# Folding a feature map into a weight matrix by halves of TensorE's rows, in a pass whose order is written out by hand

## The chip, the cores and the metric

The kernel runs on one core of a Trainium2 chip. The metric is the device time of one execution in microseconds (us). A profile shows one execution, recorded by the hardware, with an instruction's engine, start and length. The engines are TensorE (PE; its weight loads are listed apart as PEld), VectorE (DVE), ScalarE (ACT), GpSimd (POOL) and SyncE (SP), which issues most DMAs. "Lnnn" is a line of the kernel.

## What is computed

A transformer layer on x of 2048 tokens by 512 channels, in float32: a linear attention with 32 heads of 16 channels, then a token-mixing MLP (2048 to 1792 to 2048), both behind layernorms and with residuals. The change lies in the attention:

```python
q, k, v = heads of layernorm(x) @ wqkv
pq, pk  = q @ w_phi, k @ w_phi                      # a 16 x 16 matrix for each head
phi_q   = concat(softmax(pq), softmax(-pq))         # and phi_k alike
kv, z   = phi_k^T v, sum over tokens of phi_k
o       = (phi_q kv) / (phi_q z + 1e-6)
h       = x + o @ wo
out     = h + mixer(layernorm(h))
```

## The kernel before

Tokens are in 16 tiles of 128. Products that need float32 accuracy are made of parts: a matrix is split into a high part (fp32r) and the rest, and `mm3` (L69) adds three matmuls, high by high, high by low and low by high, of 128 rows by 512 moving columns each (L71, L72, L73).

**Preparation (L281 to L423).** The twelve chunks of `wT`, 128 rows each (0 to 3 for q, 4 to 7 for k, 8 to 11 for v), are loaded, and `center` (L315) takes the mean of each row out, which stands for layernorm's mean. `fold` (L332) turns a chunk around and multiplies q's and k's by phi on the way: four matmuls in plain float32 a chunk, each with 128 rows, 128 weight columns (a block of the chunk) and 128 moving columns. The moving operand `ph` (L361) is block-diagonal, with eight heads' 16 x 16 matrices on its diagonal. v's chunks are only transposed (L339). A chunk's four results fill one bank of PSUM; `hi_w` (L344, ACT at L350) copies them into the high part and `lo_w` (L352, DVE) subtracts for the low part. Chunks 0 and 1 are folded at L414 to L422, ahead of the first pass, and chunks 2 and 3 by `fold_rest` (L432) in it. Their banks come from `ps_q`, which has two and serves q's projections later.

**The first pass (L424 to L461).** For each token tile: x is loaded twice, turned (`xraw`, L111) and straight (`xh`, L116); split into parts (ACT and POOL); the row's variance is made (L129, L130 on ACT, L132 on DVE, L133 on POOL); k's projection goes to PSUM (pool `ps_k`, two banks), and DVE takes maxima, minima and two differences from it (`logit_ops`, L161); ACT does the exponentials (L195), DVE sums and reciprocals (L217, L218), POOL the products and the running sum z (L219, L223); v's projection (`ps_v`, two banks) goes through ACT (L210). After four tiles `kv` (L225) adds their products into `kvp`, in matmuls of 128 rows and 32 weight columns, so that four lie side by side in the array. q's projections and logits of six tiles are put in between.

Here the order of PE is written out: `PASSES` (L27) is a list of steps that L457 to L461 run, and each step issues one tile's k, v or q work, or f, which is `fold_rest`. Inside that block the other engines' order is chosen by the scheduler, which weighs all instructions by costs and due times of its own. Up to L423 and from L463 on, the order of the program's text holds for all engines but, in the preparation, SP.

**The rest.** From L465 the first pass ends; a second pass (L829) makes the attention's output a tile at a time: `s_tr` (L593) transposes the features in two halves of 64 rows, which alternate (L598, 64 rows, 128 weight columns, 64 moving columns), `s_num` (L609) multiplies by kv in tiles of 64 rows by 32 columns (L616), and `s_wo` follows. Then comes the mixer (L1105), which takes about half of the time.

Of the kernel before, what the change touches and what calls it, by code (L numbers as in the profile page):

```python
# [9 lines left out]
F32 = mybir.dt.float32  # L10
F32R = mybir.dt.float32r
AF = mybir.ActivationFunctionType
# [5 lines left out]
P = 128  # L18
# [24 lines left out]
def block_kernel(ctx: ExitStack, tc: tile.TileContext, x, xT, wT, phic, wo, w1, b1, w2, b2,  # L43
# [63 lines left out]
    X, XH, EQ, PK, VS, SQ, PS, W = {}, {}, {}, {}, {}, {}, {}, {}  # L107

    def load_x(t):
        raw = kk.tile([P, KD, P], F32, name="xraw", bufs=3)  # L110
# [7 lines left out]
    def split_x(t, raw, alone=False):  # L118
# [4 lines left out]
        else:  # L123
            split(X[t][:, 0], X[t][:, 1], raw, nc.gpsimd)

    def stats_x(t):
        junk = kk.tile([P, D], F32, name="sqj", bufs=1)
        st = kk.tile([P, 2], F32, name="st")
        nc.scalar.activation(junk, XH[t], AF.Copy, scale=-1.0 / D, accum_out=st[:, 0:1])  # L129
        nc.scalar.activation(junk, XH[t], AF.Square, bias=st[:, 0:1], accum_out=st[:, 1:2])  # L130
        ve = kk.tile([P, 1], F32, name="ve")
        nc.vector.tensor_scalar(ve, st[:, 1:2], 1.0 / D, EPS, op0=ALU.mult, op1=ALU.add)  # L132
        nc.gpsimd.tensor_tensor(r1[:, t:t + 1], ve, mhalf[:, :1], op=ALU.pow)  # L133
# [27 lines left out]
    def logit_ops(src, e, pool):  # L161

        v = src.rearrange("p (j h d) -> p j h d", h=2, d=DH)
        ev = signs(e)
        mx = wk.tile([P, NPR, 2], F32, name="mx")
        mn = wk.tile([P, NPR, 2], F32, name="mn")

        def shift():
            nc.vector.tensor_sub(ev[:, :, 0], v, mx.unsqueeze(3).to_broadcast([P, NPR, 2, DH]))
            if pool:  # L170
                MN.append((ev, mx, mn))
            else:
                nc.vector.tensor_sub(ev[:, :, 1], mn.unsqueeze(3).to_broadcast([P, NPR, 2, DH]), v)  # L173

        return [lambda: nc.vector.tensor_reduce(mx, v, axis=AX.X, op=ALU.max),
                lambda: nc.vector.tensor_reduce(mn, v, axis=AX.X, op=ALU.min),
                shift]

    def negate():

# [9 lines left out]
    def run(*lists):  # L190
        for op in turns(*lists):
            op()

    def exps(t, e):
        nc.scalar.activation(e, e, AF.Exp, scale=r1[:, t:t + 1])  # L195

    def heads(e):
        return e.rearrange("p g (a d) -> p (g a) d", d=DH)

    def k_ops(t, o):  # L200
        PK[t] = kk.tile([P, NG, P], F32, name="pk", bufs=PKS)
        run(logit_ops(o, PK[t], False))

    def k_logits(t):
        k_ops(t, proj(t, wkh, wkl, ps_k, "pk_ps"))
        exps(t, PK[t])

    def v_out(t, o):
        VS[t] = kk.tile([P, D], F32, name="vs", bufs=5)
# [2 lines left out]
    def v_proj(t):  # L212
        v_out(t, proj(t, wvh, wvl, ps_v, "pv"))

    def k_norm(t, z=True):
        sk = wk.tile([P, 2 * H], F32, name="sk", bufs=2)
        nc.vector.reduce_sum(sk, heads(PK[t]), axis=AX.X)  # L217
        nc.vector.reciprocal(sk, sk)  # L218
        nc.gpsimd.tensor_mul(heads(PK[t]), heads(PK[t]), sk.unsqueeze(2).to_broadcast([P, 2 * H, DH]))  # L219
        if z and t == 0:  # L220
            nc.gpsimd.tensor_copy(zacc, PK[t])
        elif z:
            nc.gpsimd.tensor_add(zacc, zacc, PK[t])  # L223

    def kv(t):  # L225

# [54 lines left out]
    with tc.tile_pool(name="prep", bufs=1) as prep:  # L281
# [50 lines left out]
        def fold(c, pool, name):  # L332
            FO[c] = pool.tile([P, KD, P], F32, name=name, tag=name)
            for kt in range(KD):
                if c < 8:
                    nc.tensor.matmul(FO[c][:, kt, :], WR[c][:, kt * P:(kt + 1) * P], ph[:, c % 4, :],
                                     start=True, stop=True)
                else:
                    nc.tensor.transpose(FO[c][:, kt, :], WR[c][:, kt * P:(kt + 1) * P], ident)  # L339
# [4 lines left out]
        def hi_w(c, vector=False, halves=1):  # L344
            n = KD // halves
            for k in range(0, KD, n):
                if vector:
                    nc.vector.tensor_copy(parts(c)[0][:, k:k + n], FO[c][:, k:k + n])
                else:
                    nc.scalar.activation(parts(c)[0][:, k:k + n], FO[c][:, k:k + n], AF.Copy)  # L350

        def lo_w(c):  # L352
            hi, lo = parts(c)
            nc.vector.tensor_sub(lo, FO[c], hi)

        warm = ps_k.tile([P, P], F32, name="pk_ps", tag="pk_ps")
        for _ in range(WARM):
            nc.tensor.matmul(warm, ones, ones, start=True, stop=True)
        with tc.manual_schedule(engines={ET.PE, ET.DVE, ET.Activation, ET.Pool}):
# [63 lines left out]
            center(3, False)  # L423
        stats_x(3)  # L424
        exps(3, PK[3])
        load_h(4)
        stats_x(4)
        k_ops(4, k4)
        exps(4, PK[4])
        v_out(2, v2)  # L430
# [7 lines left out]
        def k_step(t):  # L438

            if t + 2 < NT:  # L440
                raw = load_x(t + 2)
                load_h(t + 2)
            if t > 4:
                k_logits(t)
            k_norm(t - 1)
            if t + 2 < NT:
                split_x(t + 2, raw)
                stats_x(t + 2)

        def q_step(_):  # L450
            q_mm()
            run(q_logits(0))
            q_exp(0)
            run(q_sums(0))
# [803 lines left out]
```

## The time and the profile before

| | |
|---|---|
| time, median of 3 runs | 516.41 us (516.18 to 516.86) |
| the profiled execution's own time | 516.23 us |
| its span, first to last instruction | 514.5 us |
| preparation, on PE | to about 34 us |
| first pass, in the part that the change orders by hand | about 34 to 114 us on PE |
| second pass | about 138 to 260 us |
| mixer | to the end |

"Busy" is time in which an engine had at least one instruction running, "idle before" what it sat idle ahead of a group, with the engine or DMA that ended it. In the timeline a row begins with the start and the length in us; "x16" puts sixteen instructions that follow each other into one row. A matmul's recorded length holds the way through the array, so that the next one starts before it ends: the distance of two starts is the price of one. A matmul in plain float32 leaves two records, each with a weight load; one in fp32r and a transpose leave one.

### The profile page before, as it was taken

The numbers are of one execution on the slowest core, as the hardware profiler recorded it, in microseconds if no ns is written. First come the engines' busy times: TensorE is split into PE (matmuls) and PEld (weight loads), VectorE is DVE, ScalarE is ACT, GpSimd is POOL, SyncE is SP. The second block draws the span as 40 slices with busy tenths as digits, with TensorE's granted clock in tenths as the row PEclk, the third lists the DMA queues.
The fourth block names the chain that finished last, engine by engine and source line by source line (L and its number), as shares of the span: only waits on it lengthen the run. The fifth ranks groups of instructions, "written<-read, shape, count | busy, mean of one in ns | idle before, by whom it ended". The sixth has DMA issues, their size and how long they took to land.

```text
span 514.5 us, 10292 instructions
## 1 busy us (share of the span) xinstructions
PE 509.4 (99%) x3954; PEld 439.7 (85%) x3954; DVE 432.5 (84%) x736; ACT 300.7 (58%) x530; POOL 247.1 (48%) x195
## 2 busy tenths in 40 slices
PE   9999999999999999999999999999999999999997
PEld 8888888888877777777788999988899999999997
DVE  6799889989887899699876878986789989968973
ACT  6999853526267878867675636555364434434530
POOL 3579997876999999975203330000002112211220
PEclk9999999999999999999999999999999999999999
DMA  8642301020113233443329784333425687668743
GB/s 306 218 143 84 103 22 42 1 77 8 43 62 103 81 104 126 147 160 126 103 79 256 152 194 120 103 103 102 143 63 126 162 194 172 128 152 192 168 63 71
DMA packets 52112, 61.76 MB, mean 120 GB/s; under 512 B 4704, under 2 KB 38752, under 8 KB 52064
## 3 DMA queue, kind: packets, MB, share of 16 engines
q1 hardware_dynamic: 45440, 52.43, 32.6%
q0 software_dynamic: 6336, 8.52, 12.1%
q8 instruction: 31, 0.51, 0.4%
q10 hardware_dynamic: 288, 0.17, 0.1%
q14 instruction: 17, 0.14, 0.1%
HBM read 49.96 MB, written 11.14 MB: 119 GB/s over the span
## 4 chain that ended last, share of the span: by engine, by line
PE 95%; DVE 2%; ACT 1%; issue 0%; DVEq 0%
PE py L951 22%; PE pu L71 10%; PE pu L72 9%; PE pu L73 9%; PE py L958 9%; PE py L960 4%; PE pk_ps L71 3%; PE pk_ps L72 3%; PE pk_ps L73 3%; PE pv L73 3%; PE pv L72 3%; PE pv L71 3%; PE po L71 3%; PE po L73 2%; PE po L72 2%; PE pn L616 2%
## 5 line engine op out<-in xcount | busy, mean ns | idle before, releaser
L66 ACT ACTIVATE wp<-wraw 128x896 fp32r<-128x896 f32 (+1 forms) x96 | 79.8, 869 | 83.4 <-DVE wraw L797 34.1
L67 DVE TENSOR_TENSOR wp<-wraw,wp 128x896 fp32r<-128x896 f32 (+1 forms) x96 | 92.3, 986 | 20.7 <-ACT wp L66 20.5
L1001 POOL DMA_DIRECT2D out<-u x28 | 24.5, 952 | 170.0 <-ACT u L1047 110.8
L951 PE MATMUL py<-cb,wp 128*128 128x256 f32 x582 | 79.8, 283 | 0.0
L951 PEld LDWEIGHTS py<-cb,wp 128*128 128x128 f32 x582 | 74.0, 191 | 0.0
L490 POOL TENSOR_TENSOR ez<-eq,zB 128x1024 f32<-128x1024 f32 x16 | 38.4, 2404 | 3.8 <-ACT zB L550 3.8
L71 PE MATMUL pu<-hs,wp 128*128 128x512 f32 x96 | 37.4, 389 | 0.0
L72 PE MATMUL pu<-hs,wp 128*128 128x512 f32 x96 | 37.4, 389 | 0.0
L73 PE MATMUL pu<-hs,wp 128*128 128x512 f32 x96 | 37.3, 389 | 0.0
L219 POOL TENSOR_TENSOR pk<-pk,sk 128x1024 f32<-128x1024 f32 x16 | 31.1, 1943 | 11.3 <-DVE sk L218 10.1
L958 PE MATMUL py<-cb,wp 128*128 128x512 f32 x126 | 36.1, 394 | 0.0
L514 POOL TENSOR_TENSOR eq<-eq,w 128x1024 f32<-128x1024 f32 x16 | 32.4, 2026 | 3.5 <-DVE w L511 3.5
L223 POOL TENSOR_TENSOR zacc<-zacc,pk 128x1024 f32<-128x1024 f32 x13 | 31.3, 2406 | 0.5
L783 POOL DMA_DIRECT2D wraw<-in_w x16 | 14.2, 970 | 31.7 <-DMA wraw<-in_w 21.3
L195 ACT ACTIVATE pk<-pk,r 128x1024 f32<-128x1024 f32 x16 | 18.4, 1148 | 15.0 <-DVE pk L173 14.4
L951 PE MATMUL py<-uf,wp 128*128 128x256 f32 x198 | 26.6, 283 | 0.0
L71 PE MATMUL pu<-wq,xs 128*128 128x512 f32 x64 | 26.1, 408 | 0.0
L71 PE MATMUL pu<-hs,whl 128*128 128x512 f32 x64 | 26.0, 406 | 0.0
L71 PE MATMUL po<-woh,oh 128*128 128x512 f32 x64 | 25.3, 395 | 0.1
L72 PE MATMUL pu<-wq,xs 128*128 128x512 f32 x64 | 25.0, 391 | 0.0
L72 PE MATMUL pu<-hs,whl 128*128 128x512 f32 x64 | 25.0, 390 | 0.0
L73 PE MATMUL po<-woh,ol 128*128 128x512 f32 x64 | 25.0, 390 | 0.0
(213 smaller groups left out, 1398.5 us busy)
## 6 DMA issues: line engine op xcount, KB each, us to landing
wraw<-in_w SPq DMA_DIRECT2D x112, 256.0 KB, 3.4
out<-u POOLq DMA_DIRECT2D x21, 256.0 KB, 5.2
xraw<-in_xT SPq DMA_DIRECT2D x16, 256.0 KB, 3.0
xh<-in_x SPq DMA_DIRECT2D x16, 256.0 KB, 2.6
h<-in_x SPq DMA_DIRECT2D x16, 256.0 KB, 2.8
out<-h SPq DMA_DIRECT2D x16, 256.0 KB, 2.0
wraw<-in_wT SPq DMA_DIRECT2D x12, 256.0 KB, 5.2
wraw<-in_w POOLq DMA_DIRECT2D x16, 128.0 KB, 3.9
```

The lines of the kernel that those rows point to most:

```text
L66: nc.scalar.activation(hi, src, AF.Copy)
L67: lo_engine.tensor_sub(lo, src, hi)
L71: nc.tensor.matmul(o, ah, bh, start=first, stop=False)
L72: nc.tensor.matmul(o, ah, bl, start=False, stop=False)
L73: return nc.tensor.matmul(o, al, bh, start=False, stop=last).ins
L219: nc.gpsimd.tensor_mul(heads(PK[t]), heads(PK[t]), sk.unsqueeze(2).to_broadcast([P, 2 * H, DH]))
L223: nc.gpsimd.tensor_add(zacc, zacc, PK[t])
L490: nc.gpsimd.tensor_mul(EZ[t], EQ[t], zB)
L514: nc.gpsimd.tensor_mul(heads(EQ[t]), heads(EQ[t]), W[t].rearrange("p g c h -> p (g c h)").unsqueeze(2).to_broadcast([P, 2 * H, DH]))
L951: nc.tensor.matmul(o, w[:, m[0]], x[:, y], start=opens and i == 0, stop=closes and i == 2, skip_group_check=True)
L958: nc.tensor.matmul(o, wh_[:, m[0]], x(m[1]), start=first, stop=False, skip_group_check=True)
L1001: nc.gpsimd.dma_start(out[t * P:(t + 1) * P, k * HD:], flat(a), accum_op=ALU.add)
```

## The change

Two things are edited.

*The fold of q's chunks.* `fold_pair(c)` takes the place of `fold(c)` and `fold(c + 1)`. Because `ph` is block-diagonal, the upper 64 rows of a chunk only reach the upper 64 output columns, and the lower the lower. So each block's matmul of 128 rows by 128 moving columns becomes two of 64 rows by 64 moving columns, one for each half of the rows, with the weights 128 columns wide as before. They are issued in turn, into two banks, one for each half of the rows of both chunks. `pair_hi` and `pair_lo` copy and subtract a bank at a time; a bank now holds one half (64 columns) of both chunks, so the copies' targets are runs of 64 elements. k's fold stays as it is.

*The order.* `PASSES` goes. `FIRST` lists 285 tokens, each one operation (on one engine, but for the compound ones) of one tile, and a table `DO` maps the letter to a function; a block that orders all five engines by hand runs them. The compound functions are cut into single operations for it (`stats_x` into four, `k_norm` into four, the second difference of `logit_ops` into its own). The order that results is the one that the scheduler had chosen, for SP and POOL entirely and for DVE up to the shapes above. On PE the fold of chunks 2 and 3 (F2) now stands behind k's projection of tile 6 (k6) and not ahead of it. On ACT the copies and the centering that belong to the folds stand a few places later:

```
before: ... L210 vs#2, L350, L129 tile 5, L350, L324 chunk 3, L195 tile 3, L130 tile 5, L330 chunk 3, L129 tile 6, L195 tile 4 ...
after:  ... L210 vs#2, L129 tile 5, L195 tile 3, L130 tile 5, L350, L350, L324 chunk 3, L129 tile 6, L330 chunk 3, L195 tile 4 ...
```

The diff, cut to its core (lines of the old kernel's numbering):

```diff
-PASSES = [(s[0], int(s[1:] or 0)) for s in
-          "k5 v f k6 v q k7 q v k8 v q v q k9 k10 v k11 q k12 v k13 v q k14 v".split()]
+FIRST = """
+X5 H4 X6 a5 X7 b5 a6 b6 H5 X8 X9 s3 a7 S3 b7 a8 H6 X10 u3 b8 l4 r3 s4 m4 n2 k5 S4 o2 H7 X11 x4 y4 s5 N2 v3 u4
+p2 e3 l5 r4 S5 m5 H8 n3 s6 x5 e4 k6 F2 u5 y5 r5 S6 N3 o3 H9 n4 p3 c2 v4 u6 s7 N4 c3 d2 z2 e5 d3 l6 S7 K0 m6 K1
...
+"""
...
+        HALVES = [slice(64 * r, 64 * r + 64) for r in range(2)]
+
+        def fold_pair(c):
+
+            FO[c] = [ps_q.tile([P, 2, KD, 64], F32, name="pu", tag="pu") for _ in range(2)]
+            for i in range(2):
+                for kt in range(KD):
+                    for r, rows in enumerate(HALVES):
+                        nc.tensor.matmul(FO[c][r][:, i, kt, :], WR[c + i][rows, kt * P:(kt + 1) * P],
+                                         ph[rows, c + i, rows], start=True, stop=True, skip_group_check=True)
+
+        def pair_part(w, c, r):
+            return w[:, :, c * P:(c + 2) * P].rearrange("p k (i r f) -> p r i k f", i=2, r=2)[:, r]
+
+        def pair_hi(c, r):
+            nc.scalar.activation(pair_part(wqh, c, r), FO[c][r], AF.Copy)
+
+        def pair_lo(c, r):
+            nc.vector.tensor_sub(pair_part(wql, c, r), FO[c][r], pair_part(wqh, c, r))
...
-            fold(0, ps_q, "pu")
-            fold(1, ps_q, "pu")
+            fold_pair(0)
...
-            hi_w(0)
-            hi_w(1)
-            lo_w(0)
-            lo_w(1)
+            for r in range(2):
+                pair_hi(0, r)
+            for r in range(2):
+                pair_lo(0, r)
...
-        def fold_rest():
-            for c in range(2, 4):
-                fold(c, ps_q, "pu")
-                hi_w(c)
-                lo_w(c)
...
+        DO = {
...
+            "k": k_mm, "l": lambda t: LO_K[t][0](), "m": lambda t: LO_K[t][1](),
...
+            "j": lambda t: run(q_sum(t)), "F": fold_pair, "c": lambda c: pair_hi(c - c % 2, c % 2), "d": lambda c: pair_lo(c - c % 2, c % 2),
+        }
+        with tc.manual_schedule(engines={ET.PE, ET.DVE, ET.Activation, ET.Pool, ET.SP}):
+            for token in FIRST.split():
+                DO[token[0]](int(token[1:]))
-        with tc.manual_schedule(engines={ET.PE}):
-            k_step(3)
-            k_step(4)
-            for name, n in PASSES:
-                {"k": k_step, "v": lambda _: v_kv(), "q": q_step, "f": lambda _: fold_rest()}[name](n)
```

More of the change, by code (lines that the diff above doesn't have):

```diff
@@ L198, in heads, with logit_list @@
         return e.rearrange("p g (a d) -> p (g a) d", d=DH)
+    def logit_list(t, o):
+        PK[t] = kk.tile([P, NG, P], F32, name="pk", bufs=PKS)
+        return logit_ops(o, PK[t], False)
     def k_ops(t, o):
[L201 to L206, printed above, removed]
+        run(logit_list(t, o))
     def v_out(t, o):
@@ L213, in v_proj, with norm_sum, norm_rec, norm_mul @@
         v_out(t, proj(t, wvh, wvl, ps_v, "pv"))
-    def k_norm(t, z=True):
[L216 to L223, printed above, removed]
+    def norm_sum(t):
+        SK[t] = wk.tile([P, 2 * H], F32, name="sk", bufs=2)
+        nc.vector.reduce_sum(SK[t], heads(PK[t]), axis=AX.X)
+    def norm_rec(t):
+        nc.vector.reciprocal(SK[t], SK[t])
+    def norm_mul(t):
+        nc.gpsimd.tensor_mul(heads(PK[t]), heads(PK[t]), SK[t].unsqueeze(2).to_broadcast([P, 2 * H, DH]))
+    def norm_z(t):
+        if t == 0:
+            nc.gpsimd.tensor_copy(zacc, PK[t])
+        else:
+            nc.gpsimd.tensor_add(zacc, zacc, PK[t])
+    def k_norm(t, z=True):
+        norm_sum(t)
+        norm_rec(t)
+        norm_mul(t)
+        if z:
+            norm_z(t)
     def kv(t):
@@ new lines, in k_mm, with v_mm, q_list, hi_x @@
+        def k_mm(t):
+            LO_K[t] = logit_list(t, proj(t, wkh, wkl, ps_k, "pk_ps"))
+        def v_mm(t):
+            PV[t] = proj(t, wvh, wvl, ps_v, "pv")
+        def q_list(n):
+            q_mm()
+            EQ[n] = big.tile([P, NG, P], F32, name="eq", tag="big")
+            LO_Q[n] = logit_ops(PS[n], EQ[n], False)
+        def hi_x(t):
+            X[t] = big.tile([P, 2, KD, P], F32R, name="xs", tag="big")
+            nc.scalar.activation(X[t][:, 0], xr[t], AF.Copy)
+        DO = {
+            "X": lambda t: xr.update({t: load_x(t)}), "H": load_h,
+            "a": hi_x, "b": lambda t: nc.gpsimd.tensor_sub(X[t][:, 1], xr[t], X[t][:, 0]),
+            "s": stats_sum, "S": stats_square, "u": stats_var, "r": stats_rstd,
+            "k": k_mm, "l": lambda t: LO_K[t][0](), "m": lambda t: LO_K[t][1](),
+            "x": lambda t: LO_K[t][2](), "y": lambda t: LO_K[t][3](), "e": lambda t: exps(t, PK[t]),
+            "n": norm_sum, "N": norm_rec, "p": norm_mul, "z": norm_z,
+            "v": v_mm, "o": lambda t: v_out(t, PV[t]), "K": kv,
+            "q": q_list, "f": lambda t: LO_Q[t][0](), "g": lambda t: LO_Q[t][1](),
+            "h": lambda t: LO_Q[t][2](), "i": lambda t: LO_Q[t][3](), "E": lambda t: exps(t, EQ[t]),
+            "j": lambda t: run(q_sum(t)), "F": fold_pair, "c": lambda c: pair_hi(c - c % 2, c % 2), "d": lambda c: pair_lo(c - c % 2, c % 2),
+        }
@@ L463, in block_kernel @@
+        with tc.manual_schedule(engines={ET.PE, ET.DVE, ET.Activation, ET.Pool, ET.SP}):
+            for token in FIRST.split():
+                DO[token[0]](int(token[1:]))
+        q.update(logits=Q_EARLY, exp=Q_EARLY, sum=Q_EARLY)
+        v = NT - 4
     ms = ExitStack()
```

58 lines of the change are left out of this document (26 added, 32 removed).

## The prediction

> **What bounds the kernel now.** I read the busy times first, then the chain of work that ended last, then the list of what TensorE waited for, then the busy time by stretches, and last the timeline around the edited matmuls.
>
> ```profile
> span 514.5 us, 10292 instructions
> PE 509.4 (99%) x3954; PEld 439.7 (85%) x3954; DVE 432.5 (84%) x736; ACT 300.7 (58%) x530; POOL 247.1 (48%) x195
> ...
> PE 95%; DVE 2%; ACT 1%; issue 0%; DVEq 0%
> ```
> ```profile
> PE pk_ps L358 <- DVE eps L62: 1.1, 1, 1.1
> PE pn L616 <- DVE h L641: 0.2, 1, 0.2
> PE pu L336 <- POOL ph L361: 0.2, 1, 0.2
> ```
> ```profile
> core 0: us, PE busy (x) PEld busy (x) DVE busy (x) ACT busy (x) POOL busy (x), PEclk, DMA share, GB/s
> 30.00:130.00 100.00, 100.00 (x815) 83.33 (x814) 90.97 (x149) 61.87 (x109) 85.04 (x56) 1.00 0.18 54
> ```
>
> TensorE is busy for 509.4 of 514.5 us and makes 95% of the chain. It waits visibly three times, 1.1 + 0.2 + 0.2 = 1.5 us in all, and of these only L616 comes after the start. The written order covers TensorE's work from about 34 to 114 us; between 30 and 130 us it is never idle, at the full clock. So there is no wait in the first pass for a better order to remove. The new order can only lose; a gain can come from TensorE's own work alone, and a change in that work reaches the end as it is.
>
> **What the change does to each queue.** In the instruction order of the two programs, SP's and POOL's queues are the same, all DMAs included. DVE's are the same up to the shape of the four L354 subtractions. ACT has the same instructions, a few of them in other places between 34 and 45 us. On PE two things change. Sixteen matmuls of 128 rows by 128 moving columns (chunks 0 to 3) become 32 of 64 rows by 64 moving columns, which alternate between the two row halves. And the second pair of chunks goes behind the 12 matmuls of k's tile 6, where it stood ahead of them. That the order is written out costs and gives nothing by itself, since it writes what the scheduler had chosen.
>
> **The price of the fold now.** The timeline of PE and of its weight loads around the first pair of chunks, then the durations by line (least, median, most, in ns):
>
> ```profile
> 32.43 0.39 PE L73 MATMUL pv<-wvh,xs 128*128 128x512 f32 x1
> 32.66 1.95 PE L336 MATMUL pu<-ph,wraw 128*128 128x128 f32 x16
> 34.36 0.48 PE L71 MATMUL pk_ps<-wkh,xs 128*128 128x512 f32 x1
> 34.67 0.40 PE L72 MATMUL pk_ps<-wkl,xs 128*128 128x512 f32 x1
> ```
> ```profile
> 34.33 0.19 PEld L71 LDWEIGHTS pk_ps<-wkh,xs 128*128 128x128 f32 x1
> 34.44 0.19 PEld L72 LDWEIGHTS pk_ps<-wkl,xs 128*128 128x128 f32 x1
> ```
> ```profile
> L336 PEld LDWEIGHTS pu<-ph,wraw x48: 186/192/192, 5.1 to 41.5; 128*128 128x128 f32 x48
> L336 PE MATMUL pu<-ph,wraw x48: 270/275/347, 5.1 to 41.6; 128*128 128x128 f32 x48
> ```
>
> Eight matmuls in plain f32 leave 16 records, two passes each, and each pass has a weight load of its own. One is 275 ns long, and sixteen lie within 1.95 us, so one starts every (1.95 - 0.275)/15 = 0.112 us. From the start of the last matmul before (32.43) to the start of the second one behind (34.67) a pair costs 2.24 us. That distance I work out again for the new form. Two things could set the 112 ns: streaming 128 columns, or the weight load.
>
> **The price of the new form.** No row of before shows an f32 product on 64 rows with 128 weight columns. The nearest on one side are the transposes of L598 (64 rows, 128 weight columns, 64 moving, two halves in turn), on the other L336 itself, and kvp's L231 shows 64 moving columns in f32 in two passes.
>
> ```profile
> 138.10 0.71 PE L598 MATMUL tr<-ident,eq 64*128 64x64 f32 x16
> 138.74 0.50 PE L71 MATMUL pu<-wq,xs 128*128 128x512 f32 x1
> 139.07 0.40 PE L72 MATMUL pu<-wq,xs 128*128 128x512 f32 x1
> ```
> ```profile
> 138.09 0.57 PEld L598 LDWEIGHTS tr<-ident,eq 64*128 64x128 f32 x16
> ```
> ```profile
> L598 PEld LDWEIGHTS tr<-ident,eq x256: 135/138/140, 138.1 to 248.7; 64*128 64x128 f32 x128
> L598 PE MATMUL tr<-ident,eq x256: 221/222/272, 138.1 to 248.8; 64*128 64x64 f32 x128
> ```
> ```profile
> L339 PEld LDWEIGHTS pu<-ident,wraw x8: 138/140/142, 14.3 to 15.2; 128*128 128x128 f32 x8
> ```
> ```profile
> 46.91 0.39 PE L73 MATMUL pv<-wvh,xs 128*128 128x512 f32 x1
> 47.23 1.99 PE L231 MATMUL kvp<-pk,vs 128*32 128x64 f32 x128
> 49.15 0.50 PE L71 MATMUL pu<-wq,xs 128*128 128x512 f32 x1
> 49.49 0.40 PE L72 MATMUL pu<-wq,xs 128*128 128x512 f32 x1
> ```
> ```profile
> 49.15 0.19 PEld L71 LDWEIGHTS pu<-wq,xs 128*128 128x128 f32 x1
> 49.26 0.19 PEld L72 LDWEIGHTS pu<-wq,xs 128*128 128x128 f32 x1
> ```
> ```profile
> L231 PEld LDWEIGHTS kvp<-pk,vs x512: 106/110/110, 47.2 to 137.9; 128*32 128x32 f32 x171
> ```
> ```profile
> L616 PEld LDWEIGHTS pn<-pht,small x512: 102/107/108, 141.9 to 254.9; 64*32 64x32 f32 x171
> ```
>
> Streaming: L231 runs 128 records in groups of four, 32 groups in 1.99 us with a last record of 219 ns, (1.99 - 0.22)/31 = 57 ns a group. So 64 moving columns take half of the 112 ns, and tiles side by side share them.
>
> Weight load: a load of 128 columns is recorded at 192 ns (L336), one of 32 columns at 110 (L231). The 82 ns between them over 96 columns is 0.85 ns a column, 109 ns for 128. The timeline says the same: where nothing covers it, the next load follows after 34.44 - 34.33 and 49.26 - 49.15 = 0.11 us. And the rows that a load covers change nothing: 110 ns for 128 rows and 107 for 64 (L231, L616), 140 and 138 (L339, L598). What is cheaper is the load of a transpose, 138 against 192 ns with the same 128 columns, and so L598 gets by with a step of (0.57 - 0.138)/7 = 62 ns for a pair of halves.
>
> In the change the weights of each half are still 128 columns wide (`WR[c + i][rows, kt * P:(kt + 1) * P]`), and it is a product, not a transpose. Each half takes 16 loads for a pair of chunks, as many as the full array took. If both halves load at once, as L598's do, a step of two records takes the larger of 57 (streaming) and about 112 ns (load). I take **112 ns**; the bounds are 57 to 62 (L231, L598) below and 224 (no overlap of the two loads) above. Half the moving columns then buy nothing.
>
> What comes on top is the change of the array's shape. Into L231 the step is 47.23 - 46.91 = 0.32 us, where L336 had 0.23. The first load, 0.11, has nothing beside it. Behind L598 the last record starts at 138.10 + 0.71 - 0.22 = 138.59, L71 0.15 later, and L72 another 0.33 later.
>
> New distance for a pair: 0.32 + 0.11 + 15 x 0.112 + 0.15 + 0.33 = **2.59 us**, against 2.24: **+0.35 us**. Two pairs: **+0.70 us**.
>
> **What is moved, and who waits.** ACT's row of the last centering stands first, then the queue of the second pair's halves in before:
>
> ```profile
> 38.55 0.72 ACT L330 ACTIVATE wraw<-wraw,mu 128x512 f32<-128x512 f32 x1
> 39.17 0.63 ACT L129 ACTIVATE sqj<-xh 128x512 f32<-128x512 f32 x1
> ...
> 43.31 0.59 ACT L350 ACTIVATE wq<-pu 128x512 fp32r<-128x512 f32 x1
> ```
> ```profile
> 43.86 1.22 DVE L354 TENSOR_TENSOR wq<-pu,wq 128x512 fp32r<-128x512 f32 x2
> ```
> ```profile
> 39.90 1.95 PE L336 MATMUL pu<-ph,wraw 128*128 128x128 f32 x16
> ```
>
> The second pair started at 39.90 and needs the centered chunk 3, done at 38.55 + 0.72 = 39.27. In the new order one more L129 (0.63) stands ahead of that centering, so it is done by about 39.9. But the pair itself now starts behind k's tile 6: 39.90 + 0.35 + 12 x 0.23 (32.66 - 32.43 for one) = 43.0. Three us of cover. It ends near 43.0 + 0.1 + 0.11 + 1.68 + 0.25 = 45.1; two ACT copies with one L129 between them (0.58 + 0.83 + 0.59) and one subtraction (0.67) end near 47.8, where before the two subtractions ended at 45.1. q's first matmul with the low part, L72, stood at 49.49 and comes at 50.19: 2.4 us to spare. Behind the later subtractions DVE's k logits of tiles 5 and 6 wait up to 2.7 us. DVE has 9 us idle in 100 in that stretch, and PE does not wait for it anywhere there, so I cost this at nothing. If that cover were gone, each us that the last subtraction is later than 50.2 would stop TensorE for one us. The four copies and the four subtractions keep their 512 elements a partition, now in runs of 64; if that changes their length, the same margin covers it.
>
> **The sum.** The profiled execution took 516.23 us for a span of 514.5; it lies 0.18 below the median of 516.41. On its own time: 516.23 + 0.70 = 516.93. On the median: **517.1 us**, 0.14% longer.
>
> **The rivals.**
>
> *Halves pay off.* If a load on 64 rows takes half as long, or is hidden, the step is L598's 62 ns: 0.32 + 0.05 + 15 x 0.062 + 0.15 + 0.33 = 1.78 us, 0.46 less than now for a pair, 0.92 for both: 515.5. With L231's 57 ns and a first load of 0.03 it is 1.69, 1.1 for both: 515.3. For it: L598 does run so. Against it: L598's loads are of the cheaper kind, and no pair of rows shows a load that is shorter for fewer rows. The Trainium skill, "TensorEngine Tiling (Array Packing)", section Overview, states that a small dimension of at most 64 gives a tiling factor of 2 and a speedup of up to 2 times; by it this rival would hold, and the load rows above speak for less.
>
> *Loads in turn (the slower side).* If the loads of the two halves follow each other, there are 31 steps of 0.112 in place of 15: 4.38 us a pair, +2.14, two pairs +4.3: 520.7. Loads that overlap only in part are enough: from a step of 0.123 up the time is over 0.2% longer (0.70 + 30 x 0.011 = 1.03 us). Against it: L598's 16 loads lie in 0.57 us, two every 62 ns, though each is as long as L339's load on all 128 rows.
>
> *It doesn't do what it says.* If the halves' matmuls run one after the other but their loads overlap, two times 57 ns fill the same 112 ns: the time is that of the forecast, and only the distance of the records tells.
>
> *The written order stalls.* The second pair's late subtractions stop q's first tile (2.4 us of margin), or DVE's backlog reaches PE later. A us or two: 518 to 519.
>
> **How the numbers follow.** Load-bound forecast 0.62 (with its look-alike), halves pay off 0.22, loads in turn 0.08, stall 0.05, something near zero 0.03. The forecast's own range is 516.7 to 517.6: 10 ns a step either way make 0.3 us, the four changes of shape another 0.1 to 0.2. The range of 8 in 10 has to take in the halves that pay off, and it leaves out the loads in turn and most stalls: 515.3 to 517.8. A difference of 0.2%, 1.03 us, is about what a measurement of this kernel can tell from no change. Faster by more (below 515.4) takes the best form of the paying halves: 0.1. Slower by more (above 517.4) takes the loads in turn, the stall, or a step of 0.123 or more: 0.28. The rest, 0.62, is within.
>
> **What would show it.** In the changed kernel's timeline the fold's 32 records of a pair should lie within some 2.1 us and not 1.2; its loads should last about 190 ns and not 140; the two halves of a step should start 3 to 7 ns apart; L231's and the projections' rows should not move; PE's list of waits should stay at 1.5 us. A fold of 1.2 us, loads of 140 ns, or any new wait of PE on DVE or ACT between 30 and 130 us would prove it wrong.

## The result and the profile after

The changed kernel takes 518.0 us (median of 11 runs, 517.54 to 519.18), the kernel before, measured beside it, 516.58 (11 runs, 516.18 to 517.16). The ratio is 1.0027, 95% interval 1.0019 to 1.0035: slower by 1.42 us, where 517.1 and +0.70 were forecast. The profiled execution took 517.72 us.

The page of the changed kernel, and TensorE's list of waits:

```profile
span 515.9 us, 10354 instructions
PE 511.1 (99%) x3986; PEld 440.7 (85%) x3986; DVE 432.7 (84%) x736; ACT 300.3 (58%) x530; POOL 247.2 (48%) x195
```
```profile
PE pk_ps L411 <- DVE eps L71: 1.1, 1, 1.1
PE pn L664 <- DVE h L689: 0.2, 1, 0.2
```

TensorE is the bound as before, with 32 matmul records more and no new wait. (Its third wait in before, 0.2 us of L336 for ph, is gone.) (L80 to L82 are now what L71 to L73 were, L397 is the new fold, L369 the old one, L411 the warm-up, L264 kv.) The timeline around the first and the second pair, then L397's durations (least, median, most, in ns):

```profile
33.17 0.39 PE L82 MATMUL pv<-wvh,xs 128*128 128x512 f32 x1
33.49 2.00 PE L397 MATMUL pu<-ph,wraw 64*128 64x64 f32 x32
35.42 0.50 PE L80 MATMUL pk_ps<-wkh,xs 128*128 128x512 f32 x1
35.76 0.39 PE L81 MATMUL pk_ps<-wkl,xs 128*128 128x512 f32 x1
...
43.49 0.39 PE L82 MATMUL pk_ps<-wkh,xs 128*128 128x512 f32 x1
43.81 2.00 PE L397 MATMUL pu<-ph,wraw 64*128 64x64 f32 x32
45.74 0.50 PE L80 MATMUL pv<-wvh,xs 128*128 128x512 f32 x1
46.08 0.39 PE L81 MATMUL pv<-wvl,xs 128*128 128x512 f32 x1
```
```profile
L397 PEld LDWEIGHTS pu<-ph,wraw x64: 182/188/188, 33.5 to 45.5; 64*128 64x128 f32 x64
L397 PE MATMUL pu<-ph,wraw x64: 272/272/320, 33.5 to 45.5; 64*128 64x64 f32 x64
```

From the last matmul before to the second one behind, each pair costs 35.76 - 33.17 = 46.08 - 43.49 = 2.59 us: the forecast to the second digit, and partly by luck. The records take 1.73 us from the first start to the last, where 0.11 + 1.68 = 1.79 was forecast, and the way out (from 35.22 to L81 at 35.76) takes 0.54 us, where 0.48 was; the two misses cancel. A load of half the rows lasts 188 ns, not 140, and a step of two records takes (2.00 - 0.27)/15 = 0.115 us.

So the fold explains about half of the 1.42 us. For the rest, each matmul of one trace can be put beside the same matmul of the other, and the distance of their starts followed through the run. It grows by 0.71 us between 4.1 and 6.3 us, in instructions that are the same, by 0.73 from 8 to 45 us (the folds), and by 0.06 from there to the end. The first of these shows in the opening rows of before and after:

```profile
1.05 3.86 PE L358 MATMUL pk_ps<-ones 128*128 128x128 f32 x20 [1.05 <-DVE eps L62]
```
```profile
1.05 4.64 PE L411 MATMUL pk_ps<-ones 128*128 128x128 f32 x20 [1.05 <-DVE eps L71]
```

In both, the warm-up's matmuls start 0.21 us apart at first. In before the last six starts follow at 0.11 us, at the full clock, which begins at 3.94 us there; in after all twenty keep the slower pace, and the full clock begins at 6.36. Is that the program or chance? And does a delay of 0.73 us in the first pass reach the end as 0.73 us? The experiments answer both.

### The profile page after: what moved, and what is told of

The parts are those of the page before. It is cut to its first block, busy times and chain, and to the rows that moved or that the text cites. A ratio compares the mean times of both kernels' runs of the same rounds, so it can differ in the third digit from the quotient of the medians.

```text
span 515.9 us, 10354 instructions
## 1 busy us (share of the span) xinstructions
PE 511.1 (99%) x3986; PEld 440.7 (85%) x3986; DVE 432.7 (84%) x736; ACT 300.3 (58%) x530; POOL 247.2 (48%) x195
## 4 chain that ended last, share of the span: by engine, by line
PE 95%; DVE 2%; ACT 1%; issue 0%; DVEq 0%
PE py L999 21%; PE pu L80 10%; PE pu L81 9%; PE pu L82 9%; PE py L1006 9%; PE py L1008 4%; PE pk_ps L80 3%; PE pv L80 3%; PE pk_ps L81 3%; PE pv L81 3%; PE pk_ps L82 3%; PE pv L82 3%; PE po L80 3%; PE po L82 2%; PE po L81 2%; PE pn L664 2%
## 5 line engine op out<-in xcount | busy, mean ns | idle before, releaser
L80 PE MATMUL pu<-hs,wp 128*128 128x512 f32 x96 | 37.4, 389 | 0.0
L81 PE MATMUL pu<-hs,wp 128*128 128x512 f32 x96 | 37.4, 389 | 0.0
L82 PE MATMUL pu<-hs,wp 128*128 128x512 f32 x96 | 37.3, 389 | 0.0
L80 PE MATMUL pu<-wq,xs 128*128 128x512 f32 x64 | 26.1, 408 | 0.0
L80 PE MATMUL pu<-hs,whl 128*128 128x512 f32 x64 | 25.9, 405 | 0.0
L80 PE MATMUL po<-woh,oh 128*128 128x512 f32 x64 | 25.3, 395 | 0.1
L81 PE MATMUL pu<-wq,xs 128*128 128x512 f32 x64 | 25.0, 391 | 0.0
L81 PE MATMUL pu<-hs,whl 128*128 128x512 f32 x64 | 25.0, 390 | 0.0
L82 PE MATMUL pu<-wq,xs 128*128 128x512 f32 x64 | 25.0, 390 | 0.0
```

Of the source, the lines that this page charges most:

```text
L80: nc.tensor.matmul(o, ah, bh, start=first, stop=False)
L81: nc.tensor.matmul(o, ah, bl, start=False, stop=False)
L82: return nc.tensor.matmul(o, al, bh, start=False, stop=last).ins
```

## The experiments

**Theory:** the halves are bound by loads of 128 weight columns, the order is free, and what TensorE loses or gains is passed on to the end. **Rivals:** the order costs; the halves disturb the rest of the run; any delay is amplified further on. The runs at a glance: the difference of the medians to before, measured beside each run; the ratio with its interval (estimated from all runs and not that of the medians, so the two can differ by some tenths of a us); from the trace, the change in the distance to before's matmuls from 8 to 45 us (the edit) and from 45 us to the end (the surplus).

| run | against before, us | ratio (95%) | 8 to 45 us | behind 45 us |
|---|---|---|---|---|
| changed kernel, first | +1.42 | 1.0027 (1.0019 to 1.0035) | +0.73 | +0.06 |
| changed kernel, e4 | +1.02 | 1.0017 (1.0008 to 1.0026) | +0.68 | +0.67 |
| changed kernel, e9 | +0.96 | 1.0022 (1.0013 to 1.0030) | +0.72 | +0.90 |
| e1 order alone | -0.04 | 1.0000 (0.9991 to 1.0008) | -0.03 | -0.07 |
| e2 fold alone | +4.06 | 1.0074 (1.0061 to 1.0087) | +0.68 | +3.6 |
| e3 quarters | +0.02 | 0.9998 (0.9988 to 1.0008) | -0.97 | +1.02 |
| e5 delay 0.67 | +1.02 | 1.0021 (1.0011 to 1.0030) | +0.67 | -0.02 |
| e11 the same | +0.89 | 1.0019 (1.0011 to 1.0028) | +0.67 | +0.29 |
| e10 delay 1.79 | +2.81 | 1.0054 (1.0042 to 1.0066) | +1.78 | +0.80 |
| e6 less work | -0.92 | 0.9982 (0.9973 to 0.9991) | -0.91 | +0.10 |
| e7 quarters, early hs | -0.62 | 0.9988 (0.9978 to 0.9998) | -0.98 | +1.34 |
| e12 the same | -0.51 | 0.9996 (0.9988 to 1.0005) | -0.99 | +0.04 |
| e8 early hs alone | -0.28 | 1.0001 (0.9991 to 1.0011) | -0.01 | -0.01 |
| e13 a sum less | +0.01 | 1.0002 (0.9993 to 1.0011) | +0.01 | -0.07 |
| e14 a sum less, delay 1.79 | +1.78 | 1.0036 (1.0024 to 1.0049) | +1.82 | +0.02 |
| e15 a sum less, changed kernel | +0.81 | 1.0013 (1.0004 to 1.0021) | +0.70 | -0.03 |
| e16 a sum less, quarters, early hs | -0.91 | 0.9989 (0.9980 to 0.9998) | -0.95 | -0.02 |
| e17 quarters, sum on POOL | +6.95 | 1.0122 (1.0101 to 1.0143) | | |
| e18 old fold, sum on POOL | +8.39 | 1.0159 (1.0135 to 1.0183) | | |

### e1: the order alone

```diff
-            fold_pair(0)
+            fold(0, ps_q, "pu")
+            fold(1, ps_q, "pu")
...
-"F": fold_pair, "c": lambda c: pair_hi(c - c % 2, c % 2), "d": lambda c: pair_lo(c - c % 2, c % 2),
+"F": lambda c: [fold(c + i, ps_q, "pu") for i in range(2)], "c": hi_w, "d": lo_w,
```

> The new kernel's written order, with the old fold of 128 rows by 128 columns. Load theory (the halves are bound by their 128 weight columns, the order is free): the two folds cost what they cost before, so the run lies within 0.2 us of before, plus whatever the later grant of the full clock at the start (6.36 us into the span after, 3.94 before) adds, 0.7 us if it belongs to the new program, nothing if it changes from execution to execution. Rival 'the order costs': of the 1.42 us between the medians the folds explain 0.73, so the order alone gives +0.7 us, and the drift of PE's starts shows it inside the first pass and not ahead of 6.4 us. Rival 'halves pay off' is out already.

It equals before. The second pair behind k's tile 6, the later copies and the subtractions cost nothing, as the forecast had it. The rival is out.

### e2: the fold alone, with the scheduler

The kernel before with `fold_pair`, `pair_hi` and `pair_lo` in the places of the old functions; `PASSES` stays.

> The kernel before, its scheduler's order kept, with both pairs folded by halves. Load theory: +0.35 us for each pair, +0.7 us together against before (516.6 to 517.3), the 32 records of a pair within 2.0 us. Rival 'the order costs' says the same here, +0.7, and +0.7 for the order alone; if the order is free and the start-up is by chance, this run and the changed kernel agree within 0.2 us in the mean, so the changed kernel's +1.4 would have to come back as +0.7 to +1.4 in this run too. If the start-up delay hangs on the halves of the first fold, this run has it and the order alone has not.

Both pairs cost what they cost in the changed kernel (+0.32 to 0.35 us each, records within 2.00 us), but the run is 4 us longer. Its list of waits:

```profile
PE pk_ps L71 <- DVE pk L173: 1.5, 1, 1.5
PE pk_ps L378 <- DVE eps L62: 1.1, 1, 1.1
PE py L970 <- DVE u L1059: 0.6, 1, 0.6
PE pk_ps L568 <- DVE zl L555: 0.3, 1, 0.3
```

Between 84 and 126 us TensorE waits for differences of logits and for the sum z, and at 138 us it has lost 2.65 us more than the fold explains. The scheduler, given other instructions, had put VectorE's work in another order in 13 places, and that order is worse. Another 1.0 us goes in the mixer at 390 us, a place that comes back in e4 and e9. So the run doesn't isolate the fold as I meant it to. What it shows is what the written order does: it keeps the old order of the other engines, which the scheduler would not have kept with the new fold.

### e3: quarters

```diff
-nc.tensor.matmul(FO[c][r][:, i, kt, :], WR[c + i][rows, kt * P:(kt + 1) * P],
-                 ph[rows, c + i, rows], start=True, stop=True, skip_group_check=True)
+for h in range(2):
+    cols = slice(64 * h, 64 * h + 64)
+    nc.tensor.matmul(FO[c][r][cols, i, kt, :], WR[c + i][rows, kt * P + 64 * h:kt * P + 64 * h + 64],
+                     ph[rows, c + i, rows], start=True, stop=True, skip_group_check=True)
```

> The changed kernel with each half's matmul cut into two of 64 weight columns, so that four tiles of 64 by 64 lie side by side. Load theory: a load of 64 columns takes half as long as one of 128, about 55 ns, so a step of four records takes about 57 ns (streaming) and a pair 0.32 + 0.055 + 15 x 0.057 + 0.15 + 0.33 = 1.71 us: 0.9 us less a pair than the changed kernel, 1.8 us for both, and 0.5 less a pair than before, 1.1 for both. Rival 'streaming' (the halves' matmuls share nothing, each record costs its own 57 ns): 64 records a pair in place of 32 at the same 57 ns, a step of four takes 228 ns and a pair is 1.7 us longer than in the changed kernel, 3.5 us for both. Rival 'issue' (each instruction costs its own time whatever the tile): 64 records at 62 ns, about 4 us a pair.

The timeline around the first pair, and the durations of its line:

```profile
32.92 0.39 PE L82 MATMUL pv<-wvh,xs 128*128 128x512 f32 x1
33.24 1.16 PE L399 MATMUL pu<-ph,wraw 64*64 64x64 f32 x64
34.33 0.50 PE L80 MATMUL pk_ps<-wkh,xs 128*128 128x512 f32 x1
34.67 0.39 PE L81 MATMUL pk_ps<-wkl,xs 128*128 128x512 f32 x1
```
```profile
L399 PEld LDWEIGHTS pu<-ph,wraw x128: 129/135/135, 33.2 to 43.6; 64*64 64x64 f32 x128
```

Twice as many records in little more than half the time: a step of four takes (1.16 - 0.22)/15 = 0.063 us, a pair 34.67 - 32.92 = 1.75 us (1.71 expected). With 64 columns a load lasts 135 ns, 53 less than with 128. Rows and moving columns are those of the changed kernel; with half the weight columns, four tiles take little more than half the time of two. So neither streaming nor issue set the halves' step, and the load is what is left of the three. The rivals "streaming" and "issue" are out.

But the time is only that of before: the 0.97 us gained by 45 us are lost again. Most of it (0.66) goes at 261 us. TensorE, VectorE and ScalarE there:

```profile
261.30 0.50 PE L81 MATMUL pu<-hs,whl 128*128 128x512 f32 x1 [0.41 <-DVE hs L716]
```
```profile
258.75 0.69 DVE L734 TENSOR_TENSOR whl<-wraw,whl 128x512 fp32r<-128x512 f32 x1 [2.51 <-ACT whl L727]
259.36 1.28 DVE L76 TENSOR_TENSOR wp<-wraw,wp 128x512 fp32r<-128x512 f32 x2
260.56 0.69 DVE L716 TENSOR_TENSOR hs<-hf,hs 128x512 fp32r<-128x512 f32 x1
```
```profile
258.08 0.63 ACT L727 ACTIVATE whl<-wraw 128x512 fp32r<-128x512 f32 x1 [0.59 <-DMA wraw<-in_w]
```

Read from below: a weight load lands, ScalarE copies, VectorE subtracts that and two more and only then hs, for which TensorE waits. The load was issued 0.49 us earlier than in before, as TensorE was ahead by as much, but it took 4.02 us to land (254.04 to 258.06) and not 2.81 (254.53 to 257.34). The DMA view of just these stretches, first of before, then of e3, shows what lies inside it:

```profile
wraw<-in_w SPq DMA_DIRECT2D x1, 256.0 KB, 2.8
```
```profile
q8 instruction: 1, 0.02, 1.4%
...
wraw<-in_w SPq DMA_DIRECT2D x1, 256.0 KB, 4.0
```

One fetch of instructions on queue q8 falls into the load. That is so in all five profiles with quarters, where this load takes 3.98 to 4.06 us, and in none of the other fifteen, where it takes 2.74 to 2.97. Queue q8 makes 31 fetches of 16 KB in before, for 7908 records of TensorE and its weight loads; so a fold with 192 records more moves every fetch behind it to another place in TensorE's work, and here onto this load. No run moves a fetch alone, but the twenty profiles leave little doubt.

### e4 and e9: the changed kernel again

> The changed kernel, nothing edited. If the moment at which the full clock is granted changes from execution to execution, this profile shows another one than 6.36 us, and the ratio to before stays near 1.0027 only as a mean. If it belongs to the program, the full clock comes again near 6.4 us and the warm-up matmuls end about 0.7 us later than before's.

> The changed kernel a third time, to stand beside plain delays on the same chip. So far it is 1.47 us (means of the first 11 runs each) and 1.0 us above before, of which the folds are 0.73. Theory 'passed on': 0.73 above before, give or take 0.3 of scatter, and within 0.3 of the plain delay of 0.67. Rival 'halves disturb the rest': 0.4 or more above the plain delay.

The warm-up took 4.17 and 4.02 us in these two profiles, against 4.64 in the first and 3.86 in before, and the distance to before's matmuls at 8 us was 0.26 and -0.02 us, not 0.71. So the start belongs to the execution, not to the program: it is scatter in every kernel, and before's profile happened to have one of the shortest starts. Both runs are 1.0 us above before, and in both traces 0.66 to 0.87 us more go at one place of the mixer. First before's rows, VectorE's start of a group of weight sums and its sum u for TensorE, then the matmul that needs it:

```profile
371.75 0.69 DVE L793 TENSOR_TENSOR wraw<-wraw 128x512 f32<-128x512 f32 x1 [2.82 <-DMA wraw<-in_w]
...
389.06 0.42 DVE L1040 TENSOR_TENSOR u<-py,u 128x256 f32<-128x256 f32 x1
```
```profile
390.09 1.23 PE L951 MATMUL py<-cb,wp 128*128 128x256 f32 x9
```

VectorE is done with this sum at 389.48, 0.61 us ahead of TensorE. The same rows of e9:

```profile
373.61 0.69 DVE L841 TENSOR_TENSOR wraw<-wraw 128x512 f32<-128x512 f32 x1 [3.95 <-DMA wraw<-in_w]
...
390.91 0.42 DVE L1088 TENSOR_TENSOR u<-py,u 128x256 f32<-128x256 f32 x1
```
```profile
390.58 0.39 PE L1008 MATMUL py<-cb,wp 128*128 128x256 f32 x2
391.38 0.86 PE L999 MATMUL py<-cb,wp 128*128 128x256 f32 x5 [0.41 <-DVE u L1088]
```

TensorE was 0.70 us behind before here, but VectorE began its group 1.86 us later, when the load landed. From there to u it needs 17.3 us in both, pauses for ScalarE's copies included, and 1.86 - 0.70 = 1.16 us use up the margin of 0.61: TensorE comes 0.57 later for it, and by 0.29 more in three steps of 0.1 behind it, at matmuls whose weight load is uncovered or whose own margin is as thin.

Why did the load land late? It was issued at 366.81 us in before and at 367.53 in e9, later by what TensorE was, but took 4.82 us to land in before and 5.96 in e9. The DMA view from its issue to its landing (it and the two loads issued behind it), before and e9:

```profile
wraw<-in_w SPq DMA_DIRECT2D x3, 256.0 KB, 4.8
```
```profile
q8 instruction: 1, 0.02, 0.9%
...
wraw<-in_w SPq DMA_DIRECT2D x3, 256.0 KB, 5.9
```

It is a fetch of instructions again, which in before comes 2.65 us behind the landing (374.28). All five profiles with halves have it inside this load, which takes 5.15 to 6.12 us in them (5.15 in the changed kernel's first profile, 5.75 in e4). In the other fifteen it takes 3.4 to 5.0 us, and the fetch comes behind the landing or, in e14, in its last 0.64 us.

### e5, e11, e10: plain delays

e1's kernel; three (e5, e11) or eight (e10) of the old f32 matmuls are issued twice.

```diff
-            for kt in range(KD):
+            for kt in [0, 0, 1, 2, 3] if c < 3 else range(KD):              # e5, e11
+            for kt in [0, 0, 1, 1, 2, 2, 3, 3] if c < 2 else range(KD):     # e10
```

> The written order with the old fold, as in the first run, and three of the sixteen f32 matmuls of 128 by 128 issued twice (two ahead of the first pass, one in it): 6 records at 0.112 us, a plain delay of TensorE by 0.67 us in the place of the halves. The changed kernel is 1.2 us longer than before over all its runs (median 517.9 of 23 against 516.7 of 40), and its folds explain 0.73. Theory 'passed on': a delay reaches the end as it is, and the rest of the 1.2 is scatter of the start and of late DMAs: this run is 0.67 above before, 517.3 to 517.4. Rival 'amplified': a delay at this place makes later waits longer whatever made it, and this run too is 1.1 to 1.2 above before, 517.8 to 517.9.

> The plain delay of 0.67 us again, on the chip on which the changed kernel runs: 0.67 above before if it is passed on, and within 0.3 us of the changed kernel; 0.4 or more below the changed kernel if the halves disturb the rest of the run.

> The written order with the old fold, and all eight f32 matmuls of chunks 0 and 1 issued twice: 16 records more at 0.112 us, a delay of 1.79 us ahead of the first pass. Theory 'passed on': 1.8 above before. Rival 'amplified' (in the share of the changed kernel, 1.17 for 0.73): 2.8 above before. Rival 'a constant on top of any delay': 2.2.

A plain delay of 0.67 us costs as much as the halves: 517.91 us (median of 22 runs) against 517.83 (34 runs of the changed kernel). So the halves cost no more than a delay of their size, though the place where the surplus shows, 390 us, goes with their instructions. And 1.79 us cost 2.8, as "amplified" said; "passed on" falls for a delay of this size. In e10's trace 0.80 us more go at one place again:

```profile
405.08 0.69 DVE L842 TENSOR_TENSOR wraw<-wraw 128x512 f32<-128x512 f32 x1 [2.61 <-issue]
...
410.00 0.42 DVE L1089 TENSOR_TENSOR u<-py,u 128x256 f32<-128x256 f32 x1
```
```profile
410.47 0.74 PE L1000 MATMUL py<-cb,wp 128*128 128x256 f32 x4 [0.40 <-DVE u L1089]
```

### e6: less work

e1's kernel; in k's tile 6 the four matmuls of x's high part by the weights' low part are left out.

```diff
+        if name == "pk_ps" and t == 6:
+            for kt in range(KD):
+                nc.tensor.matmul(o, X[t][:, 0, kt, :], wh[:, kt, :], start=kt == 0, stop=False)
+                nc.tensor.matmul(o, X[t][:, 1, kt, :], wh[:, kt, :], start=False, stop=kt == KD - 1)
+            return o
```

> The written order with the old fold, and four of the twelve matmuls of k's tile 6 left out (high part of x by low part of the weights, so that tile's k lacks that term): TensorE has 0.92 us less to do at the place where the quarters saved 1.0. The quarters' fold was 1.0 us shorter in the trace, and the time was that of before. Theory 'passed on': 0.92 less, 515.8. Rival 'floor': what TensorE gains here is lost again further on, at 261 us, where L81 waits for DVE's low part of the last hs, and in the mixer, since these wait for something that does not move with TensorE: the time stays within 0.3 us of before.

-0.92 us: this gain does reach the end, so there is no floor that all kernels meet. The kernel of e6 has 4 matmuls fewer and not 96 more, and in its trace the load at 254 us takes 2.93 us. What e3 lost, it lost mostly to the load that landed late for it.

### e7, e12, e8: the last hs earlier

At the end of the second pass VectorE subtracts the last hs ahead of the mixer's first weight parts: with quarters (e7, e12) and with the old fold (e8).

```diff
+            some(DL)
             his()
             flush()
             w_parts(0)
             w_parts(1)
-            some(DL)
```

> The kernel with quarters, and at the end of the second pass DVE subtracts the last hs (L716) ahead of the weight parts of the mixer (L76) and not behind them. In the quarters' trace L81 waited 0.41 us for that subtraction at 261 us, and 0.56 of the 1.0 us gained were lost there, since a weight load landed 4.0 us after its issue and held the subtractions ahead of it. If that wait is what eats the gain, this run is 0.4 to 1.0 us shorter than the quarters (515.8 to 516.3) and no wait for hs is left. If the floor lies in the mixer, it stays at 516.7.

> The written order with the old fold, and the last hs subtracted early, as in the run before. In the trace of before that subtraction ended 0.2 us ahead of the matmul that needs it. If the wait at 261 us is a matter of chance in every kernel (the load's landing), this run is 0 to 0.3 us below before; otherwise it equals before.

> Quarters with the early hs again, beside the changed kernel on one chip. In the trace its folds take 1.0 us less than before's and the wait at 261 us is gone; the first time it was 0.62 us below before. The same again, 0.4 to 1.0 below before, and 1.5 to 1.9 below the changed kernel; what is missing of 1.0 is lost in the mixer, where single matmuls come up to 0.3 us late behind weight loads.

The wait for hs is gone, and alone the edit does nothing measurable (e8's interval holds 1). e7 and e12 give 516.34 us (median of 22 runs), 0.5 to 0.6 below before, and in e12 1.5 below the changed kernel measured beside it (e9). It is the one complete kernel whose median was in front of both, though e12's interval against before still holds 1. In e7's trace 1.34 us are lost in the mixer, at 407, 426 and 442 us; in e12's none.

### e13 to e16: a margin for VectorE in the mixer

In all four one of the four sums that VectorE makes for each weight group of the mixer is left out, so part of the second layer's weights lacks a term. e13 has the old fold, e14 e10's delay besides, e15 the halves, e16 the quarters with the early hs.

```diff
-        if plain:
-            nc.vector.tensor_add(raw[:, :, 1], raw[:, :, 1], raw[:, :, 2])
```

> The written order with the old fold, and VectorE's last sum for each weight group of the mixer left out (L845 of the changed kernel, 0.68 us, 14 times; part of the second layer's weights is wrong by it). The base for the other three. TensorE does not wait for VectorE in the mixer in the trace of before, so it should stay within 0.3 us of before; a gain of more would say that late loads reach TensorE in other executions of before too.

> The delay of 1.79 us, with that sum left out as in the run before. Theory 'VectorE's margin in the mixer': with more margin no late load reaches TensorE, no wait for u is left at 390 or 407 us, and the run is 1.8 us above the one before it. Rival 'the surplus arises elsewhere': 2.8 us above it, as without the omission.

> The changed kernel with that sum left out. Theory 'margin': 0.73 us above the base of this call, with no wait for u. Rival: 1.0 to 1.2.

> Quarters with the early hs, with that sum left out. Theory 'margin': 1.0 us below the base of this call, since the quarters' gain is no longer lost in the mixer. Rival 'the gain is lost elsewhere': 0.2 to 0.6 below.

Now a delay of 1.79 us costs 518.52 - 516.75 = 1.77, the halves 0.80, and the quarters gain 0.92. The surplus behind 45 us is zero in all four traces. In the times only the long delay is clear of the noise: by the means its surplus over 1.79 us was 0.99 us in e10 (95%: 0.46 to 1.48) and is -0.07 here (-0.42 to 0.28). The halves' 0.80 can't be told from the 1.0 of e4 and e9 by the times. VectorE's first sum u behind each group, and the matmul that needs it, in e14 at the place where e10 waited:

```profile
408.42 0.42 DVE L1087 TENSOR_TENSOR u<-py,u 128x256 f32<-128x256 f32 x1
```
```profile
409.69 0.99 PE L998 MATMUL py<-cb,wp 128*128 128x256 f32 x7
```

u is ready 0.85 us ahead, where in e10 it was 0.05, and the list of waits of e14 has no u. I took that margin, TensorE's start less the end of VectorE's sum, for the four sums behind each of the mixer's seven groups and the matmuls that need them. The smallest is 0.43 us in before (the fourth sum, L1045, done at 390.96, for the matmul at 391.39), 0.10 in the changed kernel's first profile, 0.06 in e4 and e9, 0.05 in e7 (at three groups in a row it is 0.05 to 0.06) and e10, and at least 0.68 in these four runs. So in the traces the surplus of the mixer is TensorE waiting where VectorE's margin is used up by a load that lands late.

### e17, e18: the same margin without leaving anything out

```diff
-            nc.vector.tensor_add(raw[:, :, 1], raw[:, :, 1], raw[:, :, 2])
+            nc.gpsimd.tensor_add(raw[:, :, 1], raw[:, :, 1], raw[:, :, 2])
```

> Quarters with the early hs, and the mixer's last weight sum (L845 of the changed kernel, 14 times, 0.68 us on VectorE) on GpSimd, whose only work there is to issue stores, some 0.9 us each. Theory 'margin': the gain of 1.0 us reaches the end, as with the sum left out: 0.7 to 1.0 below before, and no wait of TensorE for u. Rival 'GpSimd is too slow or its queue stands behind a store': ScalarE's copy of the group's weights, which waits for this sum, comes later, and TensorE waits for weights (wp): slower than before by 1 us or more.

> The written order with the old fold, and the same sum on GpSimd. Margin alone gains nothing where no wait is: within 0.3 us of before. If GpSimd is too slow, slower than before by as much as the quarters lose by it.

The rival was right, by more than it said. On POOL the sum takes more than twice as long (1.65 us against 0.69), ScalarE waits for it, and TensorE once for 4.53 us:

```profile
L847 POOL TENSOR_TENSOR wraw<-wraw x14: 1362/1650/1846, 359.7 to 500.8; 128x512 f32<-128x512 f32 x14
```
```profile
446.56 1.79 ACT L75 ACTIVATE wp<-wraw 128x896 fp32r<-128x896 f32 x2 [3.50 <-POOL wraw L847]
```
```profile
446.87 2.29 PE L1001 MATMUL py<-cb,wp 128*128 128x256 f32 x9 [4.53 <-DVE u L1090]
```

## Why the prediction was right, and where it was wrong

- **The price of the fold: right.** 2.59 us a pair, +0.73 together (+0.70 forecast), with two misses of 0.06 us in its parts that cancel. Loads of 188 ns, 32 records within 2.00 us, no new wait in the first pass, L264 and the projections unmoved. The term that carried it, 0.85 ns a weight column whatever the rows, is what the quarters confirm: 188 - 135 = 53 ns for 64 columns, 0.83 a column. The Trainium skill, "TensorEngine Tiling (Array Packing)", section Overview, gives a speedup of up to 2 times for a dimension of at most 64; for halves with 128 weight columns the trace has none (a step of 0.115 us against 0.112), for quarters 1.8 (0.063).
- **The moved steps at nothing: right.** e1 equals before. In the changed kernel the last subtraction of the second pair starts at 47.57 us and L81 of q's first tile at 50.95.
- **The written order "costs and gives nothing by itself, since it writes what the scheduler had chosen": right against before, incomplete.** e2 shows what the comparison hid: with the new fold the scheduler would not have chosen that order again, and its choice cost 2.65 us up to 138 us.
- **"A change in that work reaches the end as it is": the step that failed.** I took it from the first pass, where TensorE is never idle, and from a list with no waits in the mixer. The list shows waits that happened, not how near the others were. In before's profile the smallest margin is 0.43 us (at 391 us). In the fourteen profiles without an edit to the mixer's sums, the load that it hangs on is issued earlier or later with TensorE, to 0.01 us, but takes 3.6 to 6.1 us to land; where it came late by more than the margin, TensorE waited. Over e4, e9 and the two delays of 0.67 us this makes 0.28 us in the mean (95%: 0.11 to 0.44) on top of what the fold or the delay cost; at 1.79 us of delay it makes 0.99. The forecast put no term there, neither in its own range nor among the rivals. In the first profile itself the surplus is only 0.06 us, at a margin of 0.10; so for the eleven runs whose median was 518.0 this step is inferred from the later ones.
- **The base.** The forecast stood on a median of 3 runs, 516.41. Over 135 runs of before it is 516.74, since the start and the mixer scatter by some tenths in every kernel; 516.41 was low by luck. With 516.74 + 0.73 + 0.3 the sum is 517.8, where the 34 runs of the changed kernel have their median (517.83).
- **What stays open.** The first 11 runs were 0.4 us further above before than the later 23; that was not seen again, and I have no cause for it. That a fetch of instructions makes a load land late is read from twenty profiles that agree at 254 and 367 us; no run moves a fetch alone, and the waits of the delays, at 407 and 478 us or nowhere, have no account here.

## What to carry to other kernels

Before cutting a small matmul into row tiles, find out what sets its step: here it was the load of 128 weight columns, so halving rows and moving columns bought nothing, and halving the weight columns too gave 1.8 times. A list without waits does not mean margin: for each engine that feeds the bound, measure how early its result is ready, since a load that lands a microsecond late is enough to use it up. A changed number of instructions also moves the fetches of instructions, and one that falls onto a load delays it: in e3 by 1.2 us. And when a gain or loss of a microsecond doesn't come out at the end, add a plain delay of the same size: it tells at once whether the edit or the rest of the kernel is to blame.

## What the hardware showed that I had not expected

The pace of the warm-up matmuls doubles at a moment that differs from one execution to the next: the same twenty took from 3.86 to 4.64 us, and the distance to before's matmuls at 8 us is anything from -0.02 to 0.86 us in the nineteen other profiles. The full clock begins between 3.94 us (before) and 6.63 (e12), so 2.9 to 5.6 us behind the first matmul. The Trainium skill, "TensorE: Matmul & The Clock Gate", Part 1, has the transition about 4 us into sustained activity, give or take half a us between runs; these traces agree in kind, but scatter wider.

One wait can cost twice. Behind e17's idle time of 4.53 us TensorE's granted clock (the last column but two) was 0.50 for over 4 us more:

```profile
446.80:449.00 2.20, 2.13 (x10) 2.14 (x11) 1.87 (x6) 1.55 (x2) 0.00 (x0) 0.50 0.61 69
449.00:451.00 2.00, 2.00 (x7) 1.70 (x7) 2.00 (x5) 0.48 (x1) 0.86 (x1) 0.50 0.00 0
452.00:456.00 4.00, 4.00 (x31) 3.83 (x30) 2.25 (x3) 0.95 (x1) 0.00 (x0) 1.00 0.92 247
```

Against before, TensorE's matmuls came 4.7 us later by the wait, and another 2.2 us later in the three us behind, since they ran at half the pace. Of the waits of 0.4 us in the other runs none did that.
